# Global values through the sync queue, eight w_in tiles ahead of the second batch, and a new order of its pairs among the layer-one units

## The chip, the cores and the metric

The kernel runs on one core of a Trainium2 chip. The metric is the device time of one execution in microseconds; the median of several runs is compared. The engines are named as in the profile: PE is TensorE (matmuls), PEld its weight loads, DVE is VectorE, ACT is ScalarE, POOL is GpSimd, and SP is SyncE, which here only issues transfers.

## What is computed

Global-local attention for 8 batches of 8 heads, 512 local and 32 global positions, head size 64, and then a two-layer network with a hard-swish between its layers on the result. Cut to what matters:

```python
s_g = scale * q_g @ concat(k_g, k_l).T ; out_g = softmax(s_g) @ concat(v_g, v_l)
s_ll = where(abs(i - j) <= 32, scale * q_l @ k_l.T, -1e9) ; s_lg = scale * q_l @ k_g.T
out_l = softmax(concat(s_lg, s_ll)) @ concat(v_g, v_l)
x = concat(out_g, out_l)            # 8 x 544 rows of 512
h = x @ w_in                        # 512 -> 2048, "layer one"
out = (h * clip(h + 3, 0, 6) / 6) @ w_out   # 2048 -> 512, "layer two"
```

Inputs and output are float32 in memory; the kernel works in float16 with float32 sums.

## The kernel before

**Pairs.** Two heads of one batch make a pair: pair p is batch p // 4, head pair m = p % 4, 32 pairs in all. For a pair, `load` brings k, q and v into float32 staging buffers (`stg`, 16 of them, used in turn), `cast` turns them into float16, `emit_T` transposes k and q on PE and copies them out of PSUM (`copy_k` on DVE, L252; `copy_q` on ACT, L258, and a wrap of 32 columns, L267). Scores are made in windows of 128 queries against 128 keys of the pair and 32 global ones, in two halves (`ch`): `emit_S4` puts the mask into PSUM by four matmuls with the identity (L310), adds the scores (L326), and ACT takes the exponentials (L335). `emit_AV` multiplies them with the values: 16 matmuls, alternately with `vt` (L383) and with `vb` (L386), and then DVE scales by the sums (L390 and L391) into `xn`. `emit_X` transposes `xn` on PE (L444) and copies it (L448) to `xt`, the input of layer one.

**Global keys and values.** `load_g`, `cast_G` (L191, on DVE), `emit_G` (transposes `psGT` on PE, L201, and copies on DVE, L213) bring global keys ("kg") or queries ("qg") of several batches into place; `kglob` (DVE, L235) copies the keys of one batch among the local ones. The global values of a batch go into the tile `vg`: `load_vg` is a transfer that GpSimd issues and that casts on its way (L155). `vglob_m` (DVE, L228, in two halves `lo` and `hi`) copies them into `vb`, where the `vb` matmuls of AV find them. `emit_SG` makes the scores of the global queries (L357).

**Layer one and two.** A batch's 512 local rows give 16 units `u1(c)` of layer one: four matmuls of 512 columns (L472) into PSUM tile `psH`, a relu on ACT (L477, tile `t`), and one DVE instruction (L479) that writes `gt`. Units 0 to 3 need w_in tiles 0 to 3, units 4 to 7 tiles 4 to 7, and so on. Layer two (L488) follows in units of four matmuls per PSUM tile `po`. The PSUM pool has seven tiles used in turn for all of this.

**Order.** All transfers of the head stand in the SP queue in the written order; GpSimd's queue holds nearly all casts of staged tiles (L140, L174). The work of batch 0 (pairs 0 to 3) comes first, then the first units of batch 0's layer one, among which the pairs 4 to 7 of batch 1 are laid by a list of calls written out by hand. Every engine's instructions of this part are chained in program order (`pin(*ALL)`). From pair 8 on a loop lays layer-one and layer-two units among the steps of each pair; there transposes go by transfers. In that loop only the SP and GpSimd queues are chained.

Of the kernel before, what the change touches and what calls it, by code (L numbers as in the profile page):

```python
# [14 lines left out]
def kernel(  # L15
# [12 lines left out]
    nc = tc.nc  # L28
    P = 128
    B, H, Sl, D = q_l.shape  # L30
# [27 lines left out]
    def const(name, shape, dtype=FP16):  # L58
        return constp.tile(shape, dtype, tag=name, name=name)
# [12 lines left out]
    vg = const("vg", [P, B, H, D])  # L72
# [13 lines left out]
    rg = slice(D, D + Sg)  # L86
# [27 lines left out]
    def stage():  # L114
        return wrk.tile([P, 512], FP32, tag="stg", name="stg", bufs=NSTG)

    def load(p, what="kqv"):
        b, m = divmod(p, NM)
        s = st.setdefault(p, {})
        for c in what:  # L120
            src = {"k": k_l, "q": q_l, "v": v_l}[c]
            t = stage()
            if c != "v" and b < NRUN:
                nc.sync.dma_start(out=t.rearrange("p (h x) -> p h x", h=2),
                                  in_=src[b, 2 * m:2 * m + 2].rearrange("h (p j) d -> p h (j d)", j=NT))
            else:
                nc.sync.dma_start(out=t.rearrange("p (h kb d) -> p (h kb) d", h=2, kb=NT),
                                  in_=src[b, 2 * m:2 * m + 2].rearrange("h (kb p) d -> p (h kb) d", p=P))
            s[c + "f"] = t.rearrange("p (h kb d) -> p kb h d", h=2, kb=NT)

    def cast(p, what, eng):
        b, m = divmod(p, NM)
        s = st[p]
        for c in what:
            if c == "v":
                o = vts[b % NV][:, :, m, vc].rearrange("p kb (h d) -> p kb h d", h=2)
            else:
                s[c + "n"] = wrk.tile([P, NT, P], FP16, tag=c + "n", name=c + "n", bufs=4)
                o = s[c + "n"].rearrange("p kb (h d) -> p kb h d", h=2)
            eng.tensor_copy(out=o, in_=s[c + "f"])  # L140
# [13 lines left out]
    def load_vg(b):  # L154
        nc.gpsimd.dma_start(out=vg[rg, b], in_=v_g[b].rearrange("h s d -> s h d"))  # L155
# [3 lines left out]
    def load_w(kind, i):  # L159
        t = stage()  # L160
        if kind == "in":
            qd, m = divmod(i, NM)
            nc.sync.dma_start(out=t, in_=moe_w_in[m * P:(m + 1) * P, qd * 512:(qd + 1) * 512])
        else:
            nc.sync.dma_start(out=t, in_=moe_w_out[i * P:(i + 1) * P, :])
        w_st[kind, i] = t

    def cast_w(kind, i, eng):
        if kind == "in":
            qd, m = divmod(i, NM)  # L170
            o = w_in_t[m][:, qd * 512:(qd + 1) * 512]
        else:
            o = w_out_t[i // 4][:, i % 4]
        (eng.copy if eng is nc.scalar else eng.tensor_copy)(out=o, in_=w_st[kind, i])  # L174
# [5 lines left out]
    def load_g(b0, b1, nm):  # L180
        src = {"kg": k_g, "qg": q_g}[nm]
        t = stage()
        nc.sync.dma_start(
            out=t[:, 0:(b1 - b0) * HH * D].rearrange("p (n d) -> p n d", d=D),
            in_=src[b0:b1].rearrange("b (x y) s d -> (y s) (b x) d", x=HH))
        gst[b0, nm] = t

    def cast_G(b0, b1, nm, eng=nc.vector):
        n = wrk.tile([P, 4 * P], FP16, tag="gn", name=nm + "n", bufs=2)
        nb = b1 - b0  # L190
        eng.tensor_copy(out=n[:, 0:nb * P], in_=gst[b0, nm][:, 0:nb * P])  # L191
        gst[b0, nm, "n"] = n
# [22 lines left out]
    def emit_G(b0, b1, nm):  # L215
        emit_Gp(b0, b1, nm)
        for x in range(HH):
            copy_G(b0, b1, nm, x)
# [7 lines left out]
    def vglob_m(b, ms):  # L226
        n = ms.stop - ms.start
        nc.vector.tensor_copy(  # L228
            out=vbs[b % NV][rg, :, ms, vc],
            in_=vg[rg, b].rearrange("s (m h) d -> s m (h d)", h=2)[:, ms].unsqueeze(1)  # L230
            .to_broadcast([Sg, NT, n, P]))
# [30 lines left out]
    def emit_T(p):  # L262
        emit_Tp(p)
        copy_k(p)
        copy_q(p)
        s = st[p]
        nc.scalar.copy(out=s["qT"][:, 0:W].rearrange("p (i j) -> p i j", j=NT),  # L267
                       in_=s["psq"].rearrange("p (j i) -> p i j", j=NT)[:, P - W // NT:P])
# [101 lines left out]
    def emit_AV(p):  # L370
        b, m = divmod(p, NM)
        E = st[p]["E"]
        vt, vb = vts[b % NV], vbs[b % NV]
        xn = wrk.tile([P, NT, P], FP16, tag="xn", name="xn", bufs=3)
        st[p]["xn"] = xn
        for w2 in range(NT // 2):
            po = ps_tile("pav").rearrange("p (w c) -> p w c", w=2)
            for i in range(2):
                w = 2 * w2 + i
                for e in range(2):  # L380
                    o = po[:, i, e * (D + 1):(e + 1) * (D + 1)]
                    c = slice(1 + e * (D + 1), 1 + (e + 1) * (D + 1))
                    nc.tensor.matmul(out=o, lhsT=E[:, 0, e, w * P:(w + 1) * P],  # L383
                                     rhs=vt[:, w, m, c], start=True, stop=False,
                                     skip_group_check=True)
                    nc.tensor.matmul(out=o, lhsT=E[:, 1, e, w * P:(w + 1) * P],  # L386
                                     rhs=vb[:, (w - 1) % NT, m, c], start=False, stop=True,
                                     skip_group_check=True)
            rc = wrk.tile([P, 2, 2], FP32, tag="rc", name="rc", bufs=4)
            nc.vector.reciprocal(out=rc, in_=po[:, :, 0:2 * D + 2:2 * D + 1])  # L390
            nc.vector.tensor_tensor(  # L391
                out=xn[:, 2 * w2:2 * w2 + 2].rearrange("p w (e d) -> p w e d", e=2),
                in0=po[:, :, 1:1 + P].rearrange("p w (e d) -> p w e d", e=2),
                in1=rc.unsqueeze(3).to_broadcast([P, 2, 2, D]), op=mult)
# [38 lines left out]
    def emit_X(p, act=False):  # L433
        b, m = divmod(p, NM)
        xn = st[p]["xn"]
        if b > 3 or (b == 3 and m < NM - 1):
            xt = wrk.tile([P, Sl], FP16, tag=f"xt{m}", name=f"xt{m}", bufs=2)
            xts.setdefault(b, []).append(xt)
            nc.sync.dma_start_transpose(out=xt.rearrange("p (w c) -> p w c", w=NT),
                                        in_=xn.rearrange("p w c -> p (w c)"))  # L440
            return
        psX = ps_tile("psX", FP16)
        for w in range(NT):
            nc.tensor.matmul(out=psX[:, w * P:(w + 1) * P], lhsT=xn[:, w], rhs=ident,  # L444
                             is_transpose=True)
        xt = wrk.tile([P, Sl], FP16, tag=f"xt{m}", name=f"xt{m}", bufs=2)
        xts.setdefault(b, []).append(xt)
        (nc.scalar.copy if act else nc.vector.tensor_copy)(out=xt, in_=psX[:, 0:Sl])  # L448
# [84 lines left out]
    load(1, "kq")  # L533
    load_g(0, 1, "kg")
    load(2, "kq")
    load(0, "v")
    load(3, "kq")
    for p in range(1, NM):
        load(p, "v")
    for i in range(4):  # L540
        load_w("in", i)
    load_g(1, 4, "kg")
    load(4, "kq")
    for i in range(4, 8):
        load_w("in", i)
    load(5, "kq")
    load(4, "v")
    for i in range(8, 12):
# [25 lines left out]
    warm_up(17)  # L574

    make_identity(nc, ident)
    load_vg(0)
    mb = const("mb", [P, 2, P])
    ones = const("ones", [P, P])
    nc.vector.memset(ones, 1.0)  # L580
# [33 lines left out]
    def first(p, what="kqv"):  # L614
        cast(p, what, nc.gpsimd)
        vshift(p, nc.gpsimd)

    cast(1, "kq", nc.gpsimd)
    cast(2, "kq", nc.gpsimd)
    first(0, "v")  # L620
    cast(3, "kq", nc.gpsimd)
    for p in range(1, NM):
        first(p, "v")
    for i in range(4):
        cast_w("in", i, nc.gpsimd)
    cast(4, "kq", nc.gpsimd)
    load_vg(1)
    for i in range(4, 8):
        cast_w("in", i, nc.gpsimd)
    cast(5, "kq", nc.gpsimd)  # L630
    first(4, "v")
    ones_v(1, nc.gpsimd)
# [19 lines left out]
    u1 = units.pop(0)  # L652
# [39 lines left out]
    emit_X(3)  # L692
    for c in range(HEAD):
        u1(c, range(2, 3))
    cast_G(1, 4, "kg")
    for c in range(HEAD):
        u1(c, range(3, 4))
    emit_G(1, 4, "kg")
    u1(3)
    kglob(1, nc.vector)  # L700
    emit_T(4)
    u1(4)
    emit_S4(4)
    emit_T(5)
    vglob_m(1, lo)
    vglob_m(1, hi)
    u1(5)
    emit_S4(5)
    u1(6)
    emit_AV(4)  # L710
    emit_T(6)
    u1(7)
    emit_S4(6)
    emit_X(4)
    emit_AV(5)
    u1(8)
    emit_T(7)
    u1(9)
    emit_S4(7)
    emit_X(5)  # L720
    emit_AV(6)
    for t in Egs:
        nc.vector.memset(t[:, NT], 0.0)
    cast_G(0, 4, "qg")
    u1(10)
    u1(11)
    emit_AV(7)
    emit_X(6)
    emit_G(0, 4, "qg")
    u1(12)  # L730
    u1(13)
    emit_SG(0)
    emit_SG(1)
    u1(14)
    emit_TD(2 * NM)
    load(2 * NM + 1)
    cast(2 * NM + 1, "kq", nc.gpsimd)
# [158 lines left out]
```

The softmax here doesn't subtract the row's maximum and nothing guards it: scores larger than these inputs give would overflow.

## Time and profile before

| | us |
|---|---|
| median of 7 runs | 317.45 (316.8 to 317.97) |
| profiled execution | 317.45 |
| its span on the core | 315.7 |
| PE busy | 305.1 (97%) |
| DVE busy | 216.1 (68%) |
| ACT busy | 200.0 (63%) |
| POOL busy | 152.9 (48%) |

The span is counted from the core's first instruction to its last; the execution's time has 1.75 us beside it. All starts below are from the span's start. Consecutive matmuls overlap in the records, so a busy PE is not at its peak, and holes in it are found from the starts of its matmuls. In a timeline row stand the start, the length, engine, line, operation, what is written and read with sizes, how many instructions are merged, and in brackets how long the engine was idle before and what ended that.

### The profile page before, as it was taken

To read this page: it belongs to the slowest core of one execution; us is meant where nothing else is said; L and a number is where in the kernel's file an instruction comes from. 1 tells how busy PE (TensorE), PEld (TensorE's weight loads), DVE (VectorE), ACT (ScalarE), POOL (GpSimd) and SP (SyncE) were. 2 spreads that over 40 slices of the span, in tenths; PEclk is the share of its full clock that TensorE was granted. 3 is DMA by queue.
4 is the path that set the end of the run, shared out by engine and by line. 5 is a ranking of instruction groups with operands and counts; after the bars stand their busy time and mean duration, and the time that the engine had idled before them with its cause. 6 is when DMAs were issued, how large, how long until landed. Compare 5 with 4: busy or idle time off the path is not lost.

```text
span 315.7 us, 7343 instructions
## 1 busy us (share of the span) xinstructions
PE 305.1 (97%) x2688; PEld 162.6 (52%) x2688; DVE 216.1 (68%) x484; ACT 200.0 (63%) x417; POOL 152.9 (48%) x273
## 2 busy tenths in 40 slices
PE   8997899999999999999999999999999999999995
PEld 5453555545555455555555554555555544448444
DVE  5768688898665899678946996468843962479101
ACT  6856777886444984479844993589556941579000
POOL 4768997599866655773565558542411000000000
PEclk9999999999999999999999999999999999999999
DMA  7999999999999898899899999985542002100131
GB/s 222 257 304 322 299 312 327 206 205 170 247 202 239 180 212 154 172 252 158 162 151 177 201 183 199 209 200 106 113 102 86 17 19 83 66 2 1 37 98 66
DMA packets 140260, 53.05 MB, mean 168 GB/s; under 512 B 127552, under 2 KB 131904, under 8 KB 140224
## 3 DMA queue, kind: packets, MB, share of 16 engines
q1 hardware_dynamic: 138048, 52.32, 76.6%
q0 software_dynamic: 2176, 0.26, 2.2%
q8 instruction: 21, 0.34, 0.5%
q14 instruction: 15, 0.12, 0.1%
HBM read 35.13 MB, written 8.91 MB: 140 GB/s over the span
## 4 chain that ended last, share of the span: by engine, by line
PE 81%; DVE 8%; ACT 5%; issue 2%; DMA 2%; SPq 0%; POOL 0%; ACTq 0%
PE po L488 35%; PE psH L472 30%; DVE gt L479 4%; PE psS L297 3%; PE pav L383 2%; PE pav L386 2%; ACT t L477 2%; DMA stg<-in_q_l_dram 2%; DVE xn L391 2%; PE psSG L357 1%; PE psS L326 1%; ACT E L335 1%; PE po L500 1%; ACT E L301 1%; PE pg L423 1%
## 5 line engine op out<-in xcount | busy, mean ns | idle before, releaser
L488 PE MATMUL po<-wout,gt 128*128 128x512 f16 x528 | 122.6, 379 | 0.0
L472 PE MATMUL psH<-xt,win 128*128 128x512 f16 x512 | 119.8, 379 | 1.2 <-DVE gt L479 0.7
L479 DVE SCALAR_TENSOR_TENSOR gt<-t,psH 128x512 f16<-128x512 f32 (+1 forms) x144 | 90.1, 652 | 20.4 <-ACT t L477 19.1
L477 ACT ACTIVATE t<-psH,half_col 128x512 f32<-128x512 f32 (+1 forms) x144 | 92.0, 670 | 17.4 <-PE psH L472 15.5
L472 PEld LDWEIGHTS <-win 128*128 128x128 f16 x576 | 53.3, 98 | 52.8 <-POOL win L174 1.4
L488 PEld LDWEIGHTS <-gt 128*128 128x128 f16 x528 | 48.4, 98 | 52.2
L304 DVE TENSOR_TENSOR E<-E,mk 128x512 f16<-128x512 f16 x96 | 53.2, 595 | 30.1 <-ACT E L301 29.0
L301 ACT ACTIVATE E<-psS 128x512 f16<-128x512 f32 x96 | 49.8, 604 | 13.7 <-PE psS L297 13.6
L492 ACT COPY ot<-po 128x512 f32<-128x512 f32 x16 | 9.4, 586 | 58.6 <-PE po L488 46.2
L140 POOL CAST kn<-stg 128x512 f16<-128x512 f32 x31 | 19.1, 618 | 32.8 <-DMA stg<-in_k_l_dram 32.2
L409 POOL TENSOR_TENSOR s<-Eg 128x128 f32<-128x128 f16 x24 | 10.6, 443 | 36.8 <-ACT Eg L358 35.7
L391 DVE TENSOR_TENSOR xn<-pav,rc 128x256 f16<-128x256 f32 x64 | 26.1, 421 | 1.3
L492 DVE COPY ot<-po 128x512 f32<-128x512 f32 x17 | 11.7, 690 | 21.6 <-PE po L488 20.7
L140 POOL CAST vt<-stg 128x512 f16<-128x512 f32 x32 | 21.5, 671 | 10.1 <-DMA stg<-in_v_l_dram 9.6
L140 POOL CAST qn<-stg 128x512 f16<-128x512 f32 x31 | 20.6, 665 | 11.0 <-DMA stg<-in_q_l_dram 10.0
L144 POOL COPY vb<-vt 64x512 f16<-64x512 f16 x32 | 20.7, 646 | 2.1
L335 ACT ACTIVATE E<-psS 128x512 f16<-128x512 f32 x32 | 16.9, 600 | 6.4 <-PE psS L326 6.4
L383 PE MATMUL pav<-vt,E 128*128 128x65 f16 x256 | 20.1, 194 | 0.0
L386 PE MATMUL pav<-vb,E 128*128 128x65 f16 x256 | 19.9, 195 | 0.0
L383 PEld LDWEIGHTS <-E 128*128 128x128 f16 x256 | 17.9, 99 | 3.4
L386 PEld LDWEIGHTS <-E 128*128 128x128 f16 x256 | 16.8, 97 | 3.2
L297 PEld LDWEIGHTS <-kT 64*128 64x128 f16 x384 | 10.9, 94 | 9.9 <-issue 7.7
(93 smaller groups left out, 276.0 us busy)
## 6 DMA issues: line engine op xcount, KB each, us to landing
stg<-in_k_l_dram SPq DMA_DIRECT2D x32, 256.0 KB, 3.7
stg<-in_q_l_dram SPq DMA_DIRECT2D x32, 256.0 KB, 4.1
stg<-in_v_l_dram SPq DMA_DIRECT2D x32, 256.0 KB, 4.7
out_dram<-ot SPq DMA_DIRECT2D x23, 256.0 KB, 3.6
stg<-in_moe_w_in_dram SPq DMA_DIRECT2D x16, 256.0 KB, 5.6
stg<-in_moe_w_out_dram SPq DMA_DIRECT2D x16, 256.0 KB, 4.7
out_dram<-ot SPq DMA_DIRECT2D x8, 192.0 KB, 3.5
out_dram<-ot SPq DMA_DIRECT2D x16, 64.0 KB, 2.3
```

Source lines behind the costliest of these rows:

```text
L140: eng.tensor_copy(out=o, in_=s[c + "f"])
L144: eng.tensor_copy(out=vbs[b % NV][0:D, :, m, vc], in_=vts[b % NV][D:P, :, m, vc])
L301: nc.scalar.activation(out=E[:, ch, e], in_=pss[2 * ch + e], func=EXP, scale=qk_scale)
L304: nc.vector.tensor_tensor(out=E[:, ch, e], in0=E[:, ch, e], in1=mk[:, ch].rearrange("p w c -> p (w c)"), op=mult)
L383: nc.tensor.matmul(out=o, lhsT=E[:, 0, e, w * P:(w + 1) * P], rhs=vt[:, w, m, c], start=True, stop=False, skip_group_check=True)
L386: nc.tensor.matmul(out=o, lhsT=E[:, 1, e, w * P:(w + 1) * P], rhs=vb[:, (w - 1) % NT, m, c], start=False, stop=True, skip_group_check=True)
L391: nc.vector.tensor_tensor(out=xn[:, 2 * w2:2 * w2 + 2].rearrange("p w (e d) -> p w e d", e=2), in0=po[:, :, 1:1 + P].rearrange("p w (e d) ...
L472: nc.tensor.matmul(out=ps[:, 0:n], lhsT=w_in_t[m][:, c * P:(c + 1) * P], rhs=rhs(m), start=(m == 0), stop=(m == NM - 1), skip_group_check= ...
L477: nc.scalar.activation(out=t1[:, 0:n], in_=ps[:, 0:n], func=RELU, bias=half_col, scale=1.0 / 6.0)
L479: nc.vector.scalar_tensor_tensor(out=gts[c][:, 0:n], in0=t1[:, 0:n], scalar=1.0, in1=ps[:, 0:n], op0=amin, op1=mult)
L488: nc.tensor.matmul(out=po[t][:, 0:dm], lhsT=gts[c][:, t * P:(t + 1) * P], rhs=w_out_t[c // 4][:, c % 4], start=(c == 0), stop=(c == NC - 1))
L492: (nc.scalar.copy if t % 2 else nc.vector.tensor_copy)(out=ot, in_=po[t][:, 0:dm])
```

## The change

It has three parts.

1. The global values of batch 0 are no longer loaded by GpSimd. SP loads them as float32 into a staging buffer, between k and q of pair 2 and v of pair 0, and GpSimd casts them to `vg` after the casts of pair 2.
2. SP loads w_in tiles 4 to 7, and GpSimd casts them, right after tiles 0 to 3: SP ahead of the global keys of batches 1 to 3 and of k and q of pair 4, GpSimd ahead of the casts of pair 4 and of the load of global values of batch 1.
3. In the list written by hand, layer-one units 3, 4 and 5 stand ahead of the transposes of the global keys, unit 6 ahead of the scores of pair 4 and unit 7 ahead of `vglob_m`. AV of pairs 4, 5 and 6 now comes before the next unit; X of pairs 4, 5 and 6 and AV(7) move among the units as well.

```diff
     load(2, "kq")
+    vg0 = stage()
+    nc.sync.dma_start(out=vg0[rg].rearrange("s (h d) -> s h d", h=H),
+                      in_=v_g[0].rearrange("h s d -> s h d"))
     load(0, "v")
...
     for i in range(4):
         load_w("in", i)
+    for i in range(4, 8):
+        load_w("in", i)
     load_g(1, 4, "kg")
     load(4, "kq")
-    for i in range(4, 8):
-        load_w("in", i)
     load(5, "kq")
...
     make_identity(nc, ident)
-    load_vg(0)
...
     cast(2, "kq", nc.gpsimd)
+    nc.gpsimd.tensor_copy(out=vg[rg, 0], in_=vg0[rg].rearrange("s (h d) -> s h d", h=H))
     first(0, "v")
...
     for i in range(4):
         cast_w("in", i, nc.gpsimd)
+    for i in range(4, 8):
+        cast_w("in", i, nc.gpsimd)
     cast(4, "kq", nc.gpsimd)
     load_vg(1)
-    for i in range(4, 8):
-        cast_w("in", i, nc.gpsimd)
     cast(5, "kq", nc.gpsimd)
...
-    cast_G(1, 4, "kg")
     for c in range(HEAD):
         u1(c, range(3, 4))
+    u1(3)
+    u1(4)
+    cast_G(1, 4, "kg")
+    u1(5)
     emit_G(1, 4, "kg")
-    u1(3)
     kglob(1, nc.vector)
     emit_T(4)
-    u1(4)
+    u1(6)
     emit_S4(4)
     emit_T(5)
+    u1(7)
     vglob_m(1, lo)
     vglob_m(1, hi)
-    u1(5)
     emit_S4(5)
-    u1(6)
     emit_AV(4)
+    u1(8)
+    u1(9)
+    emit_X(4)
     emit_T(6)
-    u1(7)
+    u1(10)
     emit_S4(6)
-    emit_X(4)
     emit_AV(5)
-    u1(8)
+    u1(11)
     emit_T(7)
-    u1(9)
+    emit_X(5)
     emit_S4(7)
-    emit_X(5)
-    emit_AV(6)
     for t in Egs:
         nc.vector.memset(t[:, NT], 0.0)
+    emit_AV(6)
     cast_G(0, 4, "qg")
-    u1(10)
-    u1(11)
+    u1(12)
+    emit_G(0, 4, "qg")
+    u1(13)
+    emit_X(6)
     emit_AV(7)
-    emit_X(6)
-    emit_G(0, 4, "qg")
-    u1(12)
-    u1(13)
+    u1(14)
     emit_SG(0)
     emit_SG(1)
-    u1(14)
     emit_TD(2 * NM)
```

After this list both versions go on alike: X(7), unit 15, layer two.

## The prediction

> **What bounds the kernel now.** I read the page's busy shares, then busy time by stage, then TensorE's instructions in order of time, then those of VectorE and GpSimd. From the page, and from the stage table (stretch, its length, then busy time of PE, weight loads, DVE, ACT and POOL):
>
> ```profile
> PE 305.1 (97%) x2688; PEld 162.6 (52%) x2688; DVE 216.1 (68%) x484; ACT 200.0 (63%) x417; POOL 152.9 (48%) x273
> ```
>
> ```profile
> 49.50:100.00 50.50, 50.48 (x464) 26.47 (x463) 39.71 (x76) 32.60 (x76) 38.51 (x63) 1.00 1.24 229
> ```
>
> TensorE is the bound; between 49.5 and 100 us it has no idle time. So the change, which touches only what runs before 50 us, can move the end only by what TensorE gains or loses in its early holes. Starts taken against column counts (four 512-column matmuls take 0.86) give these holes between 24.3 and 48: 0.98 (layer one waits for w_in), 1.21, 0.38, 1.45 and 0.14 (scores of pairs 4 to 7) and 0.92 (first global scores), 5.1 us in all. TensorE's timeline shows the first two:
>
> ```profile
> 23.01 1.03 PE L472 MATMUL psH<-xt,win 128*128 128x512 f16 x4
> 23.87 0.39 PE L246 MATMUL psTk<-ident,kn 128*128 128x128 f16 x4
> ...
> 24.32 0.89 PE L472 MATMUL psH<-xt,win 128*128 128x512 f16 x2
> 25.38 0.39 PE L472 MATMUL psH<-xt,win 128*128 128x512 f16 x1 [0.16 <-POOL win L174]
> 25.93 0.39 PE L472 MATMUL psH<-xt,win 128*128 128x512 f16 x1 [0.17 <-POOL win L174]
> 26.16 1.03 PE L310 MATMUL psS<-mneg,ident 128*128 128x512 f16 x4
> 28.23 0.62 PE L326 MATMUL psS<-qT,kT 64*128 64x128 f16 x16 [1.04 <-DVE kT L252]
> ```
>
> Unit 4 takes one matmul per GpSimd cast; then the scores wait for VectorE, whose timeline says why:
>
> ```profile
> 22.06 0.35 DVE L191 CAST kgn<-stg 128x384 f16<-128x384 f32 x1
> 23.33 1.88 DVE L479 SCALAR_TENSOR_TENSOR gt<-t,psH 128x512 f16<-128x512 f32 x3 [0.92 <-ACT t L477]
> 25.13 1.05 DVE L213 COPY kgT<-psGT 64x192 f16<-64x192 f16 x4
> 26.22 0.69 DVE L479 SCALAR_TENSOR_TENSOR gt<-t,psH 128x512 f16<-128x512 f32 x1
> 26.82 0.75 DVE L235 COPY kT<-kgT 128x512 f16<-128x512 f16 x1
> 27.49 0.67 DVE L252 COPY kT<-psTk 128x512 f16<-128x512 f16 x1
> 28.09 0.67 DVE L479 SCALAR_TENSOR_TENSOR gt<-t,psH 128x512 f16<-128x512 f32 x1
> 29.21 0.69 DVE L252 COPY kT<-psTk 128x512 f16<-128x512 f16 x1 [0.45 <-PE psTk L246]
> 29.93 1.31 DVE L228 COPY vb<-vg 32x1024 f16<-32x1024 f16 x2
> ```
>
> VectorE executes in exactly the written order: casts and copies stand behind the gt of each layer-one unit emitted before them. Where a copy stands among the gt is what the change alters. GpSimd's timeline, the head and the stretch moved:
>
> ```profile
> 6.45 0.61 POOL L140 CAST kn<-stg 128x512 f16<-128x512 f32 x1 [3.26 <-DMA stg<-in_k_l_dram]
> 7.23 0.62 POOL L140 CAST qn<-stg 128x512 f16<-128x512 f32 x1 [0.17 <-DMA stg<-in_q_l_dram]
> ...
> 22.45 0.62 POOL L140 CAST qn<-stg 128x512 f16<-128x512 f32 x1 [0.96 <-DVE kgn L191]
> 23.01 0.59 POOL L155 DMA_DIRECT2D vg<-in_v_g_dram  x1
> 23.59 2.28 POOL L174 CAST win<-stg 128x512 f16<-128x512 f32 x4
> ```
>
> **The Trainium skill.** "Trainium Architecture — The Big Picture", section Inside one NeuronCore: each engine has its own instruction stream and meets the others only at semaphores. The trace agrees (VectorE's order above), so I walk four in-order queues. "DMA: Bandwidth & Descriptors", Issuing engines are not separate DMA queues: loads issued by SP and GpSimd share 16 DMA engines and interleave. It agrees: the page books 2.2% of 16 engines' span on GpSimd's queue, 6.9 us, 0.87 us of the whole DMA for each of eight global-value loads. "TensorE: Matmul & The Clock Gate", Back-to-back issue gap, gives 518 cycles for an isolated 512-column matmul and 131 ns sustained; here 0.86 for four, 0.216 each, decides.
>
> **Part 1, global values of batch 0.** Removed: a GpSimd-issued load (0.74 at 1.52). Added: one SP issue (0.47, as its neighbours) ahead of v of pair 0, k and q of pair 3 and all after; one staging buffer of 16; one GpSimd cast, about 0.6 (the 32x512 copy at L152 takes 0.61). The cast goes before v of pair 0, which waits 0.53 for its transfer now, so it fits into that idle time; k and q of pair 3 follow at most 0.3 later, and their transposes at 13.53 have 0.8 to spare. VectorE's copy of the values at 12.38 would find them by about 10. The SP issue hides because transfers, not issues, set arrivals (landings come about 5 us after issue). The gain is in the head: the old load runs beside k and q of pair 1, for which GpSimd waits 3.26, and the chain of waits goes from that q (7.18) through its cast and transposes to ScalarE's copy at 8.34, then on to the scores. Less competing traffic brings q up to 0.87 earlier; ScalarE, in exps from 6.92 to 8.01, can use 0.33 to 0.47 of that. I take **-0.45**, bounds 0 and -0.6. It carries on to 20 us, since no later load is then the last to come.
>
> **Part 2, w_in tiles 4 to 7.** Four SP issues (0.42 each) pass three (0.38, 0.49, 0.42), four GpSimd casts (2.28) pass two casts (0.62 each) and a load issue (0.59). The bytes are the same. w_in tile 3 is cast at 19.36; without three transfers between, four more at about 0.7 arrive by 22 to 22.8, casts done by 23.4. Unit 4 needs the last at about 24, so 0.98 goes. Late instead: q of pair 4, its arrival about 25, cast 25.6; its transpose would come near 27, so nothing. Global values of batch 1 are issued at about 25.7 rather than 23.0, landing 5.9 later (the median of that row's loads here) at about 32; VectorE wants them at 33.5. Nothing either, with 1.5 us of margin.
>
> **Part 3, the new order.** I walk the queues with rows of the trace: unit 0.86 on TensorE; relu starts 0.44 after its last matmul, lasts 0.70, next 0.58 later; gt 0.02 after relu's end, 0.60 apart; casts of global k 0.35, their copies 1.09, kglob 0.67; key copy 0.61, scores 0.74 after it starts; scores 0.55, mask matmuls 0.86, transposes 0.44, AV 0.49, X 0.22; four exps 1.92, from 0.43 after the scores start; vglob pair 1.31 (the first 0.6); scaling of an AV 1.10, from 0.45 after the AV starts. Old time base, the 0.45 taken off at the end:
>
> - Units 3, 4, 5 run without a hole from 22.8 to 25.4. The cast of global keys now stands behind gt(4), whose relu ends at 25.63: cast 26.33 to 26.68, transposes at 26.76. **Hole 1.35, new.**
> - Copies, kglob, key copy: 27.2, 28.3, 28.98; scores of pair 4 at 29.72; TensorE, with unit 6 and masks, is there at 29.09. **Hole 0.63** (was 1.21).
> - Exps of pair 4 from 30.15; q copies of pair 5 at 32.07; relu(7) 32.61 to 33.36. Scores of pair 5 at 32.83. **Hole 0.34.**
> - vglob now stands behind gt(7), at 33.39: 34.00 to 34.6. AV(4), now ahead of unit 8, reaches its first vb matmul at 33.41 and waits to 34.68. **Hole 1.27, new.**
> - Units 8, 9, X(4), transposes, unit 10, masks to 39.26; gt(9), xt(4), key copy 38.76, scores 39.50. **0.24.**
> - AV(5), unit 11, transposes, X(5), masks to 42.92; relu(11) follows the exps of pair 6, gt(11) 42.62, key copy 43.22, scores 43.96. **1.04.**
> - AV(6), unit 12 to 45.86; the cast of global queries follows the scaling of AV(6), 46.06 to 46.47. **0.67.**
> - Unit 13, X(6), AV(7), unit 14, two global scores to 49.48 without a hole. VectorE: copies to 48.86, gt(13), xt(6), scaling of AV(7) 49.81 to 50.99. X(7) takes its halves at about 50.5 and 51.05 and ends at 51.16. **About 1.5, new**, since AV(7) now lies one unit ahead of X(7) instead of three.
>
> Before, X(7) ended at 49.44 with the same work behind it: units 0 to 14, both global scores. So part 3 with part 2 costs 51.16 - 49.44 = **+1.72**; the saved 0.98 is inside it. With part 1: +1.27. After X(7), VectorE is only 0.2 later, GpSimd and DMA are not, so TensorE takes all of it to the end. The profiled execution took 317.45 (span 315.7), which is the median of the runs; 317.45 + 1.27 = **318.7**. Bounds: part 1 to zero gives 319.2; 0.1 more or less at each of the eight holes, plus or minus 0.8.
>
> **The rivals.** (a) *As walked*, slower: 0.68, own range 318.1 to 319.6. (b) *The written order does not hold on VectorE*: the program is ordered anew, and the cast of global keys goes ahead of gt(3) and vglob ahead of gt(7), where both inputs are there. The holes of 1.35 and 1.27 go: 318.7 - 2.6 = 316.1, faster. For it: near 109 us scalings and gt alternate on VectorE. Against: before 50 us the order is the written one throughout. It decides from both being early; one alone gives 317.4. Chance 0.15. (c) *Only X(7) finds its input*: if the scaling of AV(7) is done by 49.5 because the earlier holes are smaller, 1.4 goes: 317.3, no change. For it: the walk adds many steps; against: VectorE has 0.6 of idle time there. 0.17. That the new load brings no time in the head is inside (a).
>
> **How the numbers follow.** About 0.2% (0.6 us) is what a measurement of this kernel can tell from no change. Slower 0.68 from (a), same 0.17 from (c), faster 0.15 from (b). The range, 316.7 to 319.8, holds (a) and (c) and leaves out most of (b) and a walk too short by over a microsecond.
>
> **What would show it.** Right: first cast of GpSimd's k at 6.0 or earlier; no wait of unit 4 for POOL; psGT behind a DVE wait of over 1 us; an AV hole between its first vt and vb matmuls near 33; X(7) waiting for xn by over 1 us. Wrong: kgn cast before gt(3), or TensorE past X(7) before 49.4.

## The result and the profile after

| | before | after |
|---|---|---|
| median (lowest to highest), us | 317.58 (316.5 to 321.11), 63 runs | 319.93 (318.77 to 322.12), 26 runs |
| ratio | | 1.0075, 95% interval 1.0061 to 1.0090 |

The change costs 2.35 us (1.9 to 2.9), where 1.27 was forecast. The profiled execution of after took 322.0 (span 320.2) and stands near the top of its runs, so the kernel was profiled once more: that execution, **e5_again** below, took 319.43 (span 317.6), near the median of its own six runs (319.40). I read both.

The page of after, busy shares; and its stage table (stretch, length, busy time of PE, weight loads, DVE, ACT, POOL, then the clock granted to TensorE, DMA share and GB/s):

```profile
PE 306.3 (96%) x2688; PEld 162.7 (51%) x2688; DVE 213.4 (67%) x484; ACT 200.2 (63%) x417; POOL 153.2 (48%) x273
```

```profile
54.10:100.00 45.90, 45.90 (x422) 24.13 (x421) 33.99 (x66) 29.71 (x70) 33.35 (x55) 1.00 1.18 212
```

The second line is TensorE without idle time once the moved part is over, as before. From the start of unit 15 of layer one to the end of the span the three profiles take 266.39 (before), 266.13 (after) and 266.34 (e5_again): nothing changes after unit 15. All of it lies in two numbers: the start of unit 0, and from there to unit 15.

| profile | unit 0 starts | unit 0 to unit 15 | rest | span |
|---|---|---|---|---|
| before | 20.00 | 29.28 | 266.39 | 315.7 |
| after | 20.52 | 33.56 | 266.13 | 320.2 |
| e5_again | 20.15 | 31.15 | 266.34 | 317.6 |

TensorE's timeline of after, the rows that begin behind a hole (in brackets the idle time of PE and what ended it; holes are taken from start to start, so they come out a little longer):

```profile
27.26 0.34 PE L201 MATMUL psGT<-ident,kgn 128*128 128x128 f16 x3 [1.14 <-DVE kgn L191]
27.44 0.39 PE L246 MATMUL psTk<-ident,kn 128*128 128x128 f16 x4
28.56 0.40 PE L246 MATMUL psTq<-ident,qn 128*128 128x128 f16 x4 [0.73 <-POOL qn L140]
28.80 1.72 PE L472 MATMUL psH<-xt,win 128*128 128x512 f16 x4
30.31 1.91 PE L310 MATMUL psS<-mneg,ident 128*128 128x512 f16 x4
32.16 0.71 PE L326 MATMUL psS<-qT,kT 64*128 64x128 f16 x16
...
37.46 0.19 PE L386 MATMUL pav<-vb,E 128*128 128x65 f16 x1 [1.33 <-DVE vb L228]
...
49.77 0.40 PE L201 MATMUL psGT<-ident,qgn 128*128 128x128 f16 x4 [1.00 <-ACT t L477]
...
53.42 0.28 PE L444 MATMUL psX<-ident,xn 128*128 128x128 f16 x2 [0.52 <-DVE xn L391]
53.96 0.28 PE L444 MATMUL psX<-ident,xn 128*128 128x128 f16 x2 [0.26 <-DVE xn L391]
```

The waits that the walk named are here: `psGT` behind the cast of global keys, AV of pair 4 between its first `vt` and `vb` matmuls, X(7) taking its halves as they come. The rows from 28.56 to 30.31 hold what it did not name: the transposes of q of pair 4 wait for GpSimd, and then four matmuls of unit 6 take 1.72 and four of the mask 1.91, against 1.03 elsewhere. VectorE's timeline of after shows the head and the queue behind it:

```profile
10.14 0.62 DVE L223 COPY kT<-kgT 128x256 f16<-128x256 f16 x1
...
26.86 0.35 DVE L191 CAST kgn<-stg 128x384 f16<-128x384 f32 x1
...
35.93 0.69 DVE L479 SCALAR_TENSOR_TENSOR gt<-t,psH 128x512 f16<-128x512 f32 x1 [2.00 <-ACT t L477]
36.65 1.51 DVE L228 COPY vb<-vg 32x1024 f16<-32x1024 f16 x2
```

The cast and `vglob_m` stand behind a gt, as written. And GpSimd's timeline of after, the head and the stretch moved:

```profile
6.66 0.61 POOL L140 CAST kn<-stg 128x512 f16<-128x512 f32 x1 [4.47 <-DMA stg<-in_k_l_dram]
...
10.06 0.61 POOL L622 CAST vg<-stg 32x512 f16<-32x512 f32 x1
...
27.89 0.62 POOL L140 CAST qn<-stg 128x512 f16<-128x512 f32 x1 [1.70 <-PE psTk L246]
```

k of pair 1 is cast at 6.66, later than the 6.45 of before and not earlier. At 27.89 the releaser is inferred badly: the transposes it names feed nothing here, and the transfer of this q landed at 27.74.

### The profile page after: what moved, and what is told of

Same layout as the page of the kernel before. It is cut to its first block, busy times and chain, and to the rows that moved or that the text cites. A ratio compares the mean times of both kernels' runs of the same rounds, so it can differ in the third digit from the quotient of the medians.

```text
span 320.2 us, 7345 instructions
## 1 busy us (share of the span) xinstructions
PE 306.3 (96%) x2688; PEld 162.7 (51%) x2688; DVE 213.4 (67%) x484; ACT 200.2 (63%) x417; POOL 153.2 (48%) x273
## 4 chain that ended last, share of the span: by engine, by line
PE 79%; DVE 9%; ACT 6%; issue 3%; DMA 2%; SPq 0%; POOL 0%; ACTq 0%
PE po L488 35%; PE psH L472 30%; DVE gt L479 4%; PE psS L297 3%; ACT t L477 2%; PE pav L386 2%; PE pav L383 2%; ACT E L335 2%; DMA stg<-in_q_l_dram 2%; DVE xn L391 2%; PE psSG L357 1%; PE po L500 1%; ACT E L301 1%; PE pg L423 1%; PE psS L310 1%
## 5 line engine op out<-in xcount | busy, mean ns | idle before, releaser
L304 DVE TENSOR_TENSOR E<-E,mk 128x512 f16<-128x512 f16 x96 | 50.0, 559 | 31.5 <-ACT E L301 30.2
L140 POOL CAST vt<-stg 128x512 f16<-128x512 f32 x32 | 22.2, 692 | 8.0 <-DMA stg<-in_v_l_dram 7.5
```

Of the source, the lines that this page charges most:

```text
L304: nc.vector.tensor_tensor(out=E[:, ch, e], in0=E[:, ch, e], in1=mk[:, ch].rearrange("p w c -> p (w c)"), op=mult)
```

## The experiments

The theory after the result: the order of part 3 costs about what was walked, part 1 brings nothing, and single profiles add to it. The rivals: the cost is the DMAs (parts 1 and 2), or it sits in one hole and goes when that is taken away. Intervals are 95%; ratios are to the kernel before.

**e1_part1: part 1 alone.**

```diff
+    vg0 = stage()
+    nc.sync.dma_start(out=vg0[rg]..., in_=v_g[0]...)
     load(0, "v")
...
-    load_vg(0)
...
     cast(2, "kq", nc.gpsimd)
+    nc.gpsimd.tensor_copy(out=vg[rg, 0], in_=vg0[rg]...)
```

> The kernel before with part 1 alone. Theory T (the walk of the written order is right, the head was mis-sized): the q of pair 1 does not come earlier, VectorE's first copy of global keys (L223, 0.23 before) takes about 0.6 beside the new GpSimd cast, and layer one starts about 0.5 later than 20.0, so the time rises by about 0.5. Rival R1 (the head gain of the prediction stands, what is over comes from the late q of pair 4 and the halved TensorE clock): falls by 0.45. Rival R2 (a difference of transfers alone): within 0.2 of before.

Measured: 317.69, 1.0007 (0.9984 to 1.0029): none of the 0.45 is seen. q of pair 1 landed at 7.08 (before: 7.18), but layer one starts at 20.28, not 20.00: 13.15 after the cast of that q began, where in before it is 12.77. Between them lies VectorE's copy of global keys, here in its timeline for e1_part1, with GpSimd's rows of the same time below:

```profile
9.90 0.52 DVE L223 COPY kT<-kgT 128x256 f16<-128x256 f16 x1
...
10.89 0.34 DVE L223 COPY kT<-kgT 128x256 f16<-128x256 f16 x1
```

```profile
9.74 0.61 POOL L622 CAST vg<-stg 32x512 f16<-32x512 f32 x1
10.54 0.62 POOL L140 CAST vt<-stg 128x512 f16<-128x512 f32 x1 [0.20 <-DMA stg<-in_v_l_dram]
```

Both copies last 0.23 in before. The first ends at 10.42, right behind the new cast (10.35); in after the copy that starts at 10.14 ends at 10.76, behind a cast that ends at 10.67. The time rose by 0.1 where theory T expected 0.5; the interval, -0.5 to +0.9, holds both that and no change, and the forecast gain of 0.45 lies at its edge.

**e3_parts23: parts 2 and 3, with the old load.** From after:

```diff
-    vg0 = stage()
-    nc.sync.dma_start(out=vg0[rg]..., in_=v_g[0]...)
...
+    load_vg(0)
...
-    nc.gpsimd.tensor_copy(out=vg[rg, 0], in_=vg0[rg]...)
```

> The changed kernel with the old load of global values: parts 2 and 3 alone. T: the walk's +1.7, within 0.5, holes of about 1.3 at psGT, 1.3 at the first vb matmul of AV(4), 1.0 at X(7). R1: +2.8. If the q of pair 4 is late here too, a hole of up to 0.9 at its transpose and, if the clock is halved after it, up to 1.5 more in the profile.

Measured: 320.58, 1.0086 (1.0058 to 1.0114). So parts 2 and 3 make the loss; the interval of after, which has part 1 as well, overlaps this one, and no effect of part 1 can be told from the two. Unit 0 to unit 15 takes 32.08 in its profile, 0.93 more than in e5_again. One cause stands on VectorE, again beside GpSimd (e3_parts23, first VectorE's, then GpSimd's timeline):

```profile
28.71 1.28 DVE L235 COPY kT<-kgT 128x512 f16<-128x512 f16 x1
```

```profile
28.11 0.62 POOL L140 CAST kn<-stg 128x512 f16<-128x512 f32 x1
28.66 0.62 POOL L140 CAST qn<-stg 128x512 f16<-128x512 f32 x1
29.22 0.61 POOL L140 CAST vt<-stg 128x512 f16<-128x512 f32 x1
```

`kglob`, taken at 0.67 in the prediction, begins just before the first of these casts ends and lasts until the last has ended (29.83): 1.28.

**e2_part3: the order alone**, loads and casts as before. From after, beside the edit of e3_parts23:

```diff
-    for i in range(4, 8):
-        load_w("in", i)
     load_g(1, 4, "kg")
     load(4, "kq")
+    for i in range(4, 8):
+        load_w("in", i)
```

(and so with the four casts).

> The kernel before with the new order alone. T: unit 4 waits for the casts of w_in tiles 4 to 7 as before, ends at 26.15 rather than 24.55, so gt(4), the cast of global keys and psGT come 1.35 later than in the walk: +1.7 + 1.35 = +3.1. A rival (the wait for w_in runs beside the wait for the cast and is hidden): +1.7.

Measured: 321.87, 1.0119 (1.0084 to 1.0154), the slowest of all. Its TensorE waits about 0.9 in all for w_in tiles, then 1.32 for `psGT`, 1.54 at AV of pair 4 and 1.45 at X(7). By the ratio it lost 3.8 (2.7 to 4.9), where theory T had 3.1 and its rival 1.7. Without part 2 the new order reaches w_in before it is cast.

**e6_part2: part 2 alone.** The reverse edit, from before: `load_w` and `cast_w` of tiles 4 to 7 ahead of `load_g(1, 4, "kg")` and of `cast(4, "kq", ...)`.

> The kernel before with part 2 alone: w_in tiles 4 to 7 first in both queues, old order and old load of global values. T: unit 4 no longer waits, but the q of pair 4 lands near 26.7, not 22.3, and its transpose stands ahead of unit 4: TensorE waits there from 24.1 to about 27.4, 3.3, against 1.0 saved, so about +2.0 to +2.5. Rival (the gain of the removed wait shows by itself): -0.5 to -1.0.

Measured: 318.98, 1.0036 (1.0018 to 1.0055), so 0.6 to 1.7 lost, less than expected. TensorE's timeline of e6_part2:

```profile
24.25 0.34 PE L201 MATMUL psGT<-ident,kgn 128*128 128x128 f16 x3 [1.13 <-DVE kgn L191]
...
25.34 0.40 PE L246 MATMUL psTk<-ident,kn 128*128 128x128 f16 x4
27.00 0.40 PE L246 MATMUL psTq<-ident,qn 128*128 128x128 f16 x4 [1.25 <-POOL qn L140]
27.23 1.03 PE L472 MATMUL psH<-xt,win 128*128 128x512 f16 x4
```

Unit 4 (27.23, behind the transposes of pair 4) runs in one piece: the hole at w_in is gone. In its place global keys land at 23.80 (before: 20.04) and q of pair 4 is cast at 26.32. Each of parts 2 and 3 loses alone, and both together still lose.

**e5_again: after, once more.**

> The changed kernel once more, for a second profile and beside the others of this call. Theory T (the order costs 1.9 by the walk and some 0.9 more by VectorE copies that last as long as a GpSimd instruction beside them; the late q of pair 4 and the halved clock of the first profile are the exception): about +2.4 against before, no halved clock in the stretch from 25 to 35, no hole over 0.3 at the q transpose of pair 4. Rival R1 (both are there in most runs): the clock halved again near 29, span near 320.

Measured: 319.40, 1.0067 (1.0041 to 1.0092). TensorE's and VectorE's timelines of e5_again:

```profile
27.33 0.34 PE L201 MATMUL psGT<-ident,kgn 128*128 128x128 f16 x3 [1.25 <-DVE kgn L191]
...
27.73 0.39 PE L246 MATMUL psTq<-ident,qn 128*128 128x128 f16 x4
27.96 1.03 PE L472 MATMUL psH<-xt,win 128*128 128x512 f16 x4
28.82 1.03 PE L310 MATMUL psS<-mneg,ident 128*128 128x512 f16 x4
29.95 0.62 PE L326 MATMUL psS<-qT,kT 64*128 64x128 f16 x16
```

```profile
28.88 0.29 DVE L235 COPY kT<-kgT 128x512 f16<-128x512 f16 x1
...
34.35 0.75 DVE L228 COPY vb<-vg 32x1024 f16<-32x1024 f16 x2
```

q of pair 4 lands at 26.30 instead of 27.74, no transpose waits for it, the clock stays full, and the copies are short. So the same kernel took 2.4 us less here between unit 0 and unit 15: that part of the profiled execution of after belongs to that execution and not to the program.

**e4_vglob: `vglob_m` ahead of unit 7** (from after), to take the hole at AV of pair 4 away.

```diff
-    u1(7)
     vglob_m(1, lo)
     vglob_m(1, hi)
+    u1(7)
```

> The changed kernel with one edit: vglob of batch 1 ahead of unit 7, as before, not behind it. T: the hole of 1.5 between the first vt and vb matmuls of AV(4) goes, up to the landing of the global values (34.5 in the profile), and the time falls by 1.0 to 1.5 against the changed kernel, to about +1.0 against before. Rival: the hole is paid at the next scores instead, since VectorE is then late there; under 0.4 falls.

Measured: 320.23, 1.0078 (1.0058 to 1.0097): nothing gained. VectorE's and TensorE's timelines of e4_vglob:

```profile
33.52 1.52 DVE L228 COPY vb<-vg 32x1024 f16<-32x1024 f16 x2 [1.42 <-DMA vg<-in_v_g_dram]
35.07 0.69 DVE L479 SCALAR_TENSOR_TENSOR gt<-t,psH 128x512 f16<-128x512 f32 x1
```

```profile
34.77 0.19 PE L386 MATMUL pav<-vb,E 128*128 128x65 f16 x1
35.81 1.46 PE L472 MATMUL psH<-xt,win 128*128 128x512 f16 x6 [0.85 <-DVE gt L479]
```

The hole at AV shrinks from 1.5 to 0.23, and a hole of 1.01 opens at unit 8: gt of unit 7 now stands behind the copies, and with it the PSUM tile that unit 8 needs. The copies themselves wait for the global values, which land at 33.50. The rival, that the hole is only moved, came true.

**e7_kglob_act: `kglob` on ScalarE** (from after).

```diff
-    kglob(1, nc.vector)
+    nc.scalar.copy(out=kTs[1]..., in_=kgT[:, :, 1]...)
```

> The changed kernel with the copy of the global keys of batch 1 (kglob, L235) on ScalarE instead of VectorE. T: VectorE's chain from gt(4) to the key copy of pair 4 loses 0.55 to 1.3, ScalarE is idle then, the scores of pair 4 start near 29.5 and all after them that much earlier: 0.6 to 1.2 less than the changed kernel. Rival (the scores of pair 4 don't set what follows, the landing of the global values does): no difference, within 0.3.

Measured: 319.89, 1.0078 (1.0051 to 1.0105): a miss, and the rival's "no difference" came true. In its profile the copy takes 0.62 on ScalarE, from 28.93, and the copies of q stand behind it; the scores of pair 4 start at 30.17, not near 29.5, and now wait for these copies of q (L267) and no longer for VectorE. They come 9.65 after unit 0, where in e5_again it is 9.80.

**e11_kg_first: global keys early** (from after): loaded ahead of w_in 4 to 7, transposed ahead of unit 3.

```diff
+    load_g(1, 4, "kg")
     for i in range(4, 8):
         load_w("in", i)
-    load_g(1, 4, "kg")
...
+    cast_G(1, 4, "kg")
     for c in range(HEAD):
         u1(c, range(3, 4))
+    emit_G(1, 4, "kg")
     u1(3)
+    kglob(1, nc.vector)
     u1(4)
-    cast_G(1, 4, "kg")
     u1(5)
-    emit_G(1, 4, "kg")
-    kglob(1, nc.vector)
```

> The changed kernel with the global keys of batches 1 to 3 loaded ahead of w_in tiles 4 to 7, cast ahead of gt(0) and transposed ahead of unit 3, as before the change. The hole of 1.3 to 1.4 at psGT goes. T (the scores of pair 4 hang on VectorE's chain, in which gt(3) to gt(5) still stand ahead of the key copy): they start 9.45 after layer one's start instead of 9.8, and the time falls by only 0.3 to 0.4 against the changed kernel. Rival (the hole counts in full): by 1.3.

Measured: 319.41, 1.0045 (1.0023 to 1.0066), some 0.3% below after. TensorE's timeline of e11_kg_first, the scores of pair 4:

```profile
29.28 0.38 PE L310 MATMUL psS<-mneg,ident 128*128 128x512 f16 x1 [0.50 <-DVE gt L479]
30.48 0.62 PE L326 MATMUL psS<-qT,kT 64*128 64x128 f16 x16 [0.82 <-DVE kT L252]
```

`psGT` no longer waits (1.3 gone), but 0.67 (a PSUM tile that waits for its gt) and 0.99 (keys of pair 4) open before these scores.

**e8_best: the old order with three small moves** (from before): `kglob` on ScalarE, transposes of pair 4 ahead of unit 3, unit 7 ahead of the transposes of pair 6.

```diff
-    u1(3)
-    kglob(1, nc.vector)
     emit_T(4)
+    u1(3)
+    nc.scalar.copy(out=kTs[1]..., in_=kgT[:, :, 1]...)
...
-    emit_T(6)
     u1(7)
+    emit_T(6)
```

> A try for a version faster than before: the old order with kglob of batch 1 on ScalarE, the transposes of pair 4 ahead of unit 3, and unit 7 ahead of the transposes of pair 6. T: the scores of pair 4 start at about 27.0 instead of 28.2; the q of pair 6, cast at 33.4, takes back some 0.4: about -0.5 to -0.8 against before. Rival (transfers set the pace of the stretch): within 0.2 of before.

Measured: 317.99, 1.0011 (0.9994 to 1.0029): no gain. In its profiled execution, 319.89, TensorE waited 2.15 for late w_in tiles, and the clock was halved after it. From the stage tables, first e8_best, then after, then e6_part2:

```profile
24.22:27.63 3.41, 1.30 (x5) 0.26 (x3) 3.28 (x8) 2.07 (x5) 1.63 (x3) 1.00 1.20 326
27.63:31.04 3.41, 3.29 (x22) 1.44 (x23) 0.69 (x1) 1.09 (x2) 2.55 (x7) 0.50 0.98 317
```

```profile
25.57:28.98 3.41, 1.53 (x15) 0.79 (x14) 3.33 (x10) 1.26 (x2) 1.71 (x3) 1.00 1.11 314
28.98:32.40 3.42, 3.42 (x14) 1.15 (x14) 1.76 (x3) 1.36 (x3) 3.29 (x10) 0.50 1.12 337
```

```profile
23.98:27.39 3.41, 1.89 (x16) 1.04 (x17) 3.34 (x9) 1.28 (x3) 1.68 (x3) 1.00 1.11 316
```

In the first two, TensorE was busy for 1.30 and 1.53 of 3.41 us, and then ran at half clock for 3.41. In the third, the least busy such window of e6_part2 before its end, it was busy for 1.89 and the clock stayed full. How the windows are chosen is explained further down.

**e9_loads: three more GpSimd loads in the head** (from before), to measure what such a load costs k and q of pair 1.

```diff
+    for b in (1, 2, 3):
+        load_vg(b)
```

> The suspected cost of the old load, four times: the kernel before, with three more loads of global values (batches 1 to 3, as later loads bring again) issued by GpSimd in the head after the masks. The step of the prediction (each such load takes 0.5 to 0.87 of the whole DMA from k and q of pair 1 and of the pairs behind it): q of pair 1 lands 1.3 to 2.6 later, or the loads after it, layer one starts at 21.3 to 22.5 and the time rises by 1.3 or more. Theory T (such a load takes almost nothing from the transfers beside it): q of pair 1 lands between 7.2 and 8.2 as in the other profiles with the old load, under +0.5.

Measured: 318.37, 1.0026 (1.0007 to 1.0045). GpSimd's timeline of e9_loads:

```profile
3.19 1.77 POOL L155 DMA_DIRECT2D vg<-in_v_g_dram  x3
...
6.56 0.62 POOL L140 CAST qn<-stg 128x512 f16<-128x512 f32 x1 [0.23 <-DMA stg<-in_q_l_dram]
```

q of pair 1 landed at 6.51, not later than the 7.18 of before. Later transfers moved back: v of pair 0 from 10.14 to 10.96, q of pair 3 from 11.71 to 12.54. Three such loads cost 0.26% (0.8 us, 0.2 to 1.4), more than the 0.5 of theory T at the middle and less than the 1.3 of the other side; in this profile none of it falls on k and q of pair 1.

**e10_cast_late: part 1, its cast behind the cast and shift of v of pair 0.** Beside the load of e1_part1:

```diff
     first(0, "v")
+    nc.gpsimd.tensor_copy(out=vg[rg, 0], in_=vg0[rg]...)
     cast(3, "kq", nc.gpsimd)
```

> Part 1 alone, with the GpSimd cast of the global values behind v of pair 0 and its shift instead of ahead of them. T: VectorE's first L223 copy meets no running GpSimd instruction and takes 0.23 again, and from the landing of the q of pair 1 to the start of layer one it is 12.7 to 12.8, not 13.2 as in three of the profiles with part 1. The time is within 0.3 of before. Rival (the copy is slow for another reason): 0.5 to 0.6 and 13.2.

Measured: 317.37, 0.9998 (0.9977 to 1.0019). VectorE's and GpSimd's timelines of e10_cast_late:

```profile
10.31 0.23 DVE L223 COPY kT<-kgT 128x256 f16<-128x256 f16 x1
...
11.00 0.54 DVE L223 COPY kT<-kgT 128x256 f16<-128x256 f16 x1
```

```profile
10.84 0.62 POOL L140 CAST vt<-stg 128x512 f16<-128x512 f32 x1 [0.68 <-DMA stg<-in_v_l_dram]
```

The first copy is short again; the second now meets the cast of v, and ends behind it. In this profile the conflict moved and did not go: unit 0 still starts 13.11 after the cast of q began, so that part of the expectation failed. But the first copy is short as soon as the cast beside it is gone, which its rival, a slow copy for another reason, did not allow.

**e12_u14: the kernel before, with unit 14 ahead of the global scores**, into its hole of 0.92.

```diff
+    u1(14)
     emit_SG(0)
     emit_SG(1)
-    u1(14)
```

> One piece of the new order alone: the kernel before with unit 14 ahead of the two global scores. T (walk): unit 14 fills the wait of 0.92 for the copies of the global queries, all after it comes 0.86 earlier: about -0.8 against before, 316.8. Rival (X(7) or the next copies wait instead): within 0.3 of before.

Measured: 317.18, 0.9983 (0.9965 to 1.0001). Busy time by stage, first e12_u14, then before:

```profile
47.00:52.00 5.00, 5.00 (x44) 2.52 (x43) 4.91 (x11) 4.06 (x11) 3.81 (x8) 1.00 1.05 242
```

```profile
47.00:52.00 5.00, 4.24 (x41) 2.33 (x40) 4.45 (x12) 3.87 (x10) 3.51 (x7) 1.00 1.18 318
```

The hole is filled and unit 15 starts 1.22 earlier, at 48.06; but from there to the end it takes 267.64 instead of 266.39 and the span is the same 315.7. In this profile the gain holds until 105 and goes in one hole: at 106.46 TensorE has been idle for 1.08, waiting for a gt. That gt stands behind multiplications of exponentials with the mask on VectorE (L304, float16 in SBUF), which run beside a copy of global values on GpSimd. VectorE's and GpSimd's timelines of e12_u14, then VectorE's of before:

```profile
103.11 2.58 DVE L304 TENSOR_TENSOR E<-E,mk 128x512 f16<-128x512 f16 x3
```

```profile
102.24 2.09 POOL L147 COPY vb<-vg 32x2048 f16<-32x2048 f16 x1
```

```profile
104.37 1.51 DVE L304 TENSOR_TENSOR E<-E,mk 128x512 f16<-128x512 f16 x3
```

In before that copy of GpSimd ended at 101.23, ahead of these multiplications. Whether the gain goes the same way in the runs without a profile isn't shown. Of all versions run this one came nearest to beating before, at the edge of what the runs can tell.

## Why the prediction was right and where it was wrong

The direction was right, and the walk held. By its own steps, holes in us from start to start:

| step | predicted | after | e5_again |
|---|---|---|---|
| unit 4, for w_in tile 7 | 0 | 0 | 0.35 |
| `psGT` behind the cast of global keys | 1.35 | 1.31 | 1.42 |
| transposes of q of pair 4 | 0 | 0.90 | 0 |
| unit 6 to scores of pair 4, over 8 matmuls of 0.216 | 0.63 | 1.63 (half clock) | 0.26 |
| scores of pair 5 | 0.34 | 0.38 | 0.38 |
| AV of pair 4, for `vb` | 1.27 | 1.51 | 1.17 |
| scores of pair 6; of pair 7 | 0.24; 1.04 | 0.21; 1.01 | 0.20; 1.01 |
| `psGT` of global queries | 0.67 | 1.16 | 1.03 |
| X(7) | 1.5 | 1.11 | 1.12 |

The walk reached unit 15 at 51.16, 31.16 after unit 0; e5_again has 31.15. So VectorE executes the written order, and the rival that it does not is gone; X(7) does wait, so the rival "no change" is gone too. A small slip stands in the sum: 51.16 was set against 49.44, the end of X(7) in the records, while unit 15 of before started at 49.28. On one footing the walk gives +1.88, not +1.72.

The forecast of +1.27 was short of the measured 2.35 by 1.1: 0.45 for a gain that did not come, 0.16 for the slip, and some 0.5 beyond the walk.

**The step that failed is the gain in the head, -0.45.** It argued that the load issued by GpSimd takes DMA time from k and q of pair 1. e1_part1, without that load, shows no gain (+0.1); e9_loads, with three more, has that q no later. Over the 14 profiles of this study it lands at 6.5 to 8.2, a spread larger than the gain supposed, and the median is 7.28 in the seven with the old load and 7.40 in the seven without. The other way round, the added cast, costed at nothing since GpSimd had idle time for it, took time from VectorE: unit 0 starts 12.6 to 12.8 after the cast of q of pair 1 began where both copies of global keys take 0.23, and 13.1 to 13.2 where a GpSimd instruction runs when one of them begins and lengthens it (after, e1_part1, e7_kglob_act, e10_cast_late, e11_kg_first), so 0.4 in the profiles that show it. (e9_loads, whose later transfers are late, has 12.99.) The cover named, GpSimd's idle time, was real; what it missed is a second user of the same ports. The Trainium skill, "SBUF — State Buffer", section Who interferes with whom, says that VectorE copies in the two-port mode and GpSimd contend for one pair of ports, and that the one which starts first holds it for its whole instruction. The traces agree: 0.62 instead of 0.23 with a cast running, 0.23 with none. That it is not GpSimd's work as such is seen from VectorE's copies out of PSUM (L213): over the 14 profiles they take 0.18 to 0.30 with a GpSimd instruction running as without.

**The second mis-sized term is the fixed length of VectorE's copies.** `kglob` entered at 0.67 and lasted 0.29 (e5_again), 0.55 (after) and 1.28 (e3_parts23), by what GpSimd had begun; the `vglob_m` pair entered at 1.31 and lasted 0.75 to 1.55. That the walk ended within 0.02 of e5_again is luck, since its errors cancelled: shorter copies and a shorter wait at X(7), against a wait of 0.35 for w_in tile 7, which landed at 24.10 and not by 22.8, and a cast of global queries that took 0.77 beside GpSimd instead of 0.41.

**The third is q of pair 4.** Its arrival of 25 was 26.3 in e5_again, where it still fits, and 27.7 in after. There it cost 0.90, and it lies close behind the hole of 1.31 at `psGT`; then the clock fell, and unit 6 and the mask at half clock cost 1.37 more than in e5_again. The global values behind it, walked to 32, landed at 33.83 in e5_again and 34.48 in after; `vglob_m` began at 34.35 and 36.65, so this cost nothing, but most of the margin of 1.5 was gone in e5_again. The Trainium skill, "TensorE: Matmul & The Clock Gate", section What's actually happening, says that the clock falls to half after an idle window of about 3.4 us and that the windows run freely. The length agrees: the half clock lasted 3.41. The idleness does not: TensorE was busy for 1.53 of the 3.41 us before it.

Where the windows lie can be read from the traces. In all 14 profiles a stretch at full clock lasts 7, 84, 91 or 92 times 3.413 us, so windows of 3.413 us can be counted from the moment at which the clock became full: 5.09 in after, 3.7 to 7.0 in all. Of the 1278 such windows at full clock, 16 were followed by half clock, 14 of them at the end of the program. In these TensorE was busy for 0 to 1.53 us; in all others for 1.61 or more (the least is e4_vglob, 313.38 to 316.79). e6_part2, with holes of 1.29 and 1.42 close together, kept the full clock: its least busy window before the end has 1.89. So the busy time within one window tells the two kinds apart in every case on record, and where the windows fall differs between executions of the same kernel. No run moved a hole against the windows on purpose.

The half clock is not in the difference of the medians. The clock granted in each run is on record: its mean is 0.993 to 0.995 in three of the 26 runs of after (322.0, 321.28 and 322.12) and 0.998 or more in the others, whose median is 319.91. Among 143 runs of before made beside the experiments, 14 have 0.992 to 0.995, as large a share.

The sum of what was measured: the order +1.88 by the walk and +1.87 in e5_again; the head +0.1 by the runs of e1_part1 (-0.5 to +0.9). The measured 2.35 (1.9 to 2.9) lies 0.1 to 1.0 above the walk. The candidates that the profiles show are copies that meet GpSimd: 0.4 in the head, and between unit 0 and unit 15 up to the 0.93 that e3_parts23 took more than e5_again, with a `kglob` that was 0.99 longer. How often they fall in the runs that were not profiled can't be told, so the split of this rest stays open.

## What to carry to other kernels

An order written for one engine is also an order for every engine that feeds it: a copy put behind one more elementwise step is late by that step's own wait, and taking away one such hole (e4_vglob, e7_kglob_act, e11_kg_first) mostly showed the next in line. Walk all queues before moving work; a walk of four queues with durations from a trace found every hole but one of e5_again, each within 0.4 us, and the close fit of the total was luck. And before an instruction is costed at nothing because its engine is idle, see which instructions run beside it on the other engine, and how much the arrivals of transfers vary between executions of the same kernel. A hole filled early can be lost later in the same way, as e12_u14 shows.

## What the hardware showed that was not expected

- A float16 instruction of VectorE in SBUF that begins while GpSimd is running can last until that instruction has ended: the copies L223 and L235 that were held up so ended 0.08 to 0.16 after it, the halves of `vglob_m` about 0.28 after it, and `kglob` sat through two more casts that followed (1.28 instead of 0.29). The multiplications of L304 take 0.41 to 0.43 with no GpSimd instruction running and 0.82 in the median, at most 2.08, with one running.
- TensorE's clock was halved for 3.41 us inside the program in two of 14 profiles, after windows of 3.413 us in which TensorE was busy for 1.30 (e8_best) and 1.53 (after); no window with 1.61 or more was followed by half clock.
- Transfers of the same kernel landed up to 1.4 us apart in two executions (q of pair 4: 26.30 and 27.74).
